# A one-element GpSimd copy that releases three held stores moves from in front of the last gather to behind it

## The chip, the cores and the metric

The kernel runs on one core of a Trainium2 chip. The metric is the device time of one execution in microseconds (us). Engines are named as in the profile: PE (TensorE matmul) and PEld (its weight load), DVE (VectorE), ACT (ScalarE), POOL (GpSimd) and SP (SyncE, which issues plain DMAs). A name with q behind it, as POOLq, is the engine's sequencer. Times on the axis of the trace count from the start of the span.

## The reference

Two layers, for 4 batches of 6208 tokens with 256 channels, in float32:

```
sig = 1 / (1 + exp(-f_logit))
f   = lower_bound + (1 - lower_bound) * sig
h_t = f_t * h_(t-1) + (1 - f_t) * x_t           # a scan over the tokens, per channel
y   = all h_t

scores = y @ w_gate                              # per batch: the 128 tokens of the highest score
h   = relu(y[top] @ w1)                          # 256 -> 1024
out = y;  out[top] = y[top] + sigmoid(scores[top]) * (h @ w2)
```

## The kernel before, in words

Tokens lie along the free axis and channels on the partitions. A batch is cut into units of up to four blocks of 256 tokens; there are 25 units, numbered 0 to 24, and batch 3 ends with unit 24. For each unit SP loads the gate logits and x, ACT makes the gates, POOL and DVE weigh x, DVE runs the scan, PE adds up the scores and turns the result so that tokens stand on partitions, ACT and DVE copy it out of PSUM into a tile `ym`, and SP stores this tile (1 MB for a unit of four blocks) to the output of its batch, line 446.

After the last unit of a batch its 128 best tokens are searched. Then comes the batch's expert step: a **gather** by indirect DMA on POOL (`fetch`, line 657) reads the chosen rows back from the output in device memory into `xe`; PE transposes them (line 685); the gate is a dot product on DVE (line 707); up matmuls (line 718 for the last batch, 727 for others), a relu on ACT (line 735), down matmuls (740, for the last batch 745), the mix with the gate on DVE (752, for the last batch two halves, 749), and a **scatter** by indirect DMA on POOL (line 756) that writes the rows back. The gather has to wait until the stores of its rows have landed, and the scatter until all stores of its batch have.

The stores of the last two units of batches 0 and 1 (units 5, 6, 11 and 12) are **held**: the stores of all other units go first. The gathers of these two batches leave out the rows of held units and take these from the tiles on the chip, so only the scatters of batches 0 and 1 wait for the held stores: batch 0's for unit 6, batch 1's for unit 12. `stored` is the order of all stores, `unheld` its first part. Unit 5 is the first of the held, and it is issued right behind unit 24's store. Units 6, 11 and 12 wait in addition for `("passed",)`. That is a copy of one element of unit 6's `ym` tile onto itself, on POOL: SP's next store reads this tile, so it waits for the copy, and the two behind it in SP's order wait with it.

The order on each engine is written by a planner (`Plan.run`) before the kernel is built. Each operation is given to it by `add(engine, cost, emit, rank, after, key, ...)`; of the operations that are ready on an engine the planner takes the smallest rank, at times that it works out from the costs. Here `p0` is 20 times the batch's last unit plus a constant of the batch, which is larger for batch 3 than for the batches before it; the scatter of batch 2 has a smaller rank than the copy and the gather of batch 3. The conditions (`after`) order the plan alone; on the chip an instruction waits for the tiles and tensors that it reads and writes. The copy is given the conditions of the last gather, the landing of unit 24's store among them, but it touches no more than its one element.

Before the last gather POOL also writes one element of each of batch 3's tiles (`see`, line 642) and so waits for the stores of units 19 to 23. The planner allows for the gather's landing on its own account, with `LAND[3]` = 1.85 and 0.36 for the queue, and 0.055 from one engine to the next. In the stretch between batch 2's matmuls and the down matmuls of the last batch the planner fills idle PE time with matmuls that nobody reads (line 967, `FILL` = 0.24 each), one for as long as more than 1.1 x `FILL` is free before the next real operation.

After the last batch's gate the engines read a flag and branch (lines 881 to 883): the usual case goes on with the same plan, the other case would search again. The scatters of batches 0, 1 and 3 stand behind this branch, in this order, and batch 2's ahead of it.

Of the kernel before, what the change touches and what calls it, by code (L numbers as in the profile page):

```python
# [53 lines left out]
HELD = [2, 2, 0, 0]  # L54
# [19 lines left out]
class Plan:  # L74
# [8 lines left out]
    def add(self, engine, cost, emit, rank, after, key=None, late=0.0, takes=(), load=1.0, over=None, behind=None, bank=()):  # L83
        if key is not None:
            self.at[key] = len(self.ops)
        if behind:
            self.behind[len(self.ops)] = behind
        self.bank[len(self.ops)] = [(name[:-2], name[-1] == "w") for name in ([bank] if isinstance(bank, str) else bank)]
        over = OVER.get(engine, 0.0) if over is None else over
        self.ops.append((engine, cost, emit, rank, [k for k in after if k is not None], late, takes, load * (cost - over), over))  # L90
# [179 lines left out]
def gated_scan_moe(tc, xf, heads_in, lbwg, w12, outs, cap):  # L270
    nc = tc.nc
    v, a, pe, g = nc.vector, nc.scalar, nc.tensor, nc.gpsimd
    with ExitStack() as ctx:
# [49 lines left out]
        for k in range(OWN):  # L323

            first = max(0, min(4, RANKED - 4 * k)) * LANE
# [18 lines left out]
        N = len(units)  # L344
        last_unit = {u[0]: i for i, u in enumerate(units)}
        first_unit = {u[0]: i for i, u in reversed(list(enumerate(units)))}
        held = {i for b in range(B) for i in range(last_unit[b] - HELD[b] + 1, last_unit[b] + 1)}
        unheld = [i for i in range(N) if i not in held]
        stored = unheld + sorted(held)
        before = dict(zip(stored[1:], stored))  # L350
        plan = Plan(SLOTS, CAPS)
        add = plan.add
        xs, fs, gs, pts, yms, wide, chosen, carry, aim, spelt = {}, {}, {}, {}, {}, {}, {}, {}, {}, {}
# [409 lines left out]
        def experts(b):  # L763
            st = {}
            fetch, turn_in, take, ask, opened, up, relu, down, mix, scatter = stages(b, st)
            turn_half, take_half, up_half, down_half, mix_half, copy_indices, see = st["half"]
            halved = b == B - 1
            p0 = 20.0 * last_unit[b] + EXPERT[b]
            k = lambda *t: ("moe", b, *t)

            prev = ("mix", b - 1)
            if halved:
                add("pool", 0.19, copy_indices, p0, [("st", b)], ("index", b))
                for i in range(last_unit[b - 1] + 1, N - 1):
                    add("pool", 0.17, lambda i=i: see(i), p0, [("store", i), ("store", "tail", b), ("index", b), ("seen", i - 1)], ("seen", i))
            ahead = [("st", b), ("index", b), ("seen", N - 2) if halved else None, ("store", last_unit[b] - HELD[b]), ("store", "tail", b)]
            if halved and len(stored) > len(unheld) + 1:
                first = stored[len(unheld) + 1]
                add("pool", 0.12, lambda: g.tensor_copy(yms[first][:1, 0, :1], yms[first][:1, 0, :1]), p0, ahead, ("passed",))
                ahead = [*ahead, ("passed",)]  # L780
            add("pool", 1.1, fetch, p0, ahead, k("fetch"))
            add("sw", 0.36, None, p0 - 1e3, [k("fetch")], k("row" if HELD[b] else "xe"), late=LAND[b])
            if HELD[b]:
                spell, broadcast, match, pick, join = st["held"]
# [9 lines left out]
            if halved:  # L794
                plan.tile(("pm", b, -1), ("pt", "pt"), [("xT", b, 1)])
                for h in range(NH):
                    add("pe", 0.272, lambda h=h: turn_half(h), p0 - 2, [k("xe"), ("moe", b - 1, "down", NF - 1), k("flip", h - 1)], k("flip", h), takes=[("pm", b, -h)], load=0.7, over=0.12)
                    add("dve" if h else "act", 0.28, lambda h=h: take_half(h), p0 - 2, [k("flip", h)], ("xT", b, h) if h else ("xT", b))
            else:
                add("pe", 0.438, turn_in, p0, [k("xe"), ("moe", b - 1, "down", NF - 1)], k("flip"), takes=[("pm", b, 0)], load=0.7, over=0.13)  # L800
                add("act", 0.375, take, p0 - 1, [k("flip")], ("xT", b))
# [174 lines left out]
        first = [("scores", first_unit[b], 0) for b in range(B)]  # L976
# [16 lines left out]
        for b in range(B):  # L993
            choose(b)
            experts(b)
# [37 lines left out]
```

## Time and profile before

| | |
|---|---|
| median of 3 runs | 208.09 us (207.54 to 208.29) |
| profiled execution | 207.37 us, of which the span is 205.5 us |
| mean granted clock of PE | 0.988 |
| PE, DVE, ACT, POOL busy | 183.3, 161.0, 155.8, 142.0 us |
| DMA | 79.64 MB, mean 388 GB/s |

The span runs from the first to the last instruction of the traced execution; the time of an execution is a little longer than its span. Busy time is the time in which an engine worked on instructions; the DMA figures count the packets of the core's 16 DMA engines. Idle time of an engine costs nothing where another sets the pace.

### The profile page before, as it was taken

The page shows a single profiled execution, that of the slowest core. Times are in us where ns is not written, and L with a number is a line of the kernel's source. Part 1 is how long each engine was busy: PE and PEld are TensorE (multiplying, and loading weights), DVE is VectorE, ACT ScalarE, POOL GpSimd, SP SyncE. Part 2 cuts the span into 40 slices and gives each one's busy share as a digit, 9 for nine tenths or more (in the row PEclk, how much of TensorE's full clock was granted, in tenths as well). Part 3 has the DMA queues.
Part 4 walks back from the last instruction along what each step waited for, and adds up shares of the span by engine and source line. Part 5 has one row for each costly group of instructions (what it writes and reads, how often), then busy time and mean ns, then how long its engine had stood idle before and what let it go on. Part 6 is the DMA issues. An engine that isn't in the chain of part 4 may idle for free. (4 is left out here: it accounts for less than half of the span.)

```text
span 205.5 us, 4047 instructions
## 1 busy us (share of the span) xinstructions
PE 183.3 (89%) x1561; PEld 136.8 (67%) x1561; DVE 161.0 (78%) x194; ACT 155.8 (76%) x205; POOL 142.0 (69%) x142
## 2 busy tenths in 40 slices
PE   5799999889798979999999999989989999990990
PEld 3577667566565757679876668769857666780990
DVE  0959999995998899999979999999999988500110
ACT  2788899967989968979999999997999983310210
POOL 5203996745999999994999999749969950322301
PEclk9999999999999999999999999999999999999698
DMA  5999999999999999999999999999999999999101
GB/s 191 390 443 427 427 401 444 427 429 427 411 423 418 420 442 409 438 419 421 418 442 407 427 405 429 413 435 416 437 426 405 427 427 425 420 419 389 64 26 35
DMA packets 9799, 79.64 MB, mean 388 GB/s; under 512 B 1329, under 2 KB 1597, under 8 KB 2736
## 3 DMA queue, kind: packets, MB, share of 16 engines
q1 hardware_dynamic: 9248, 78.39, 91.2%
q0 software_dynamic: 384, 0.95, 1.2%
q8 instruction: 14, 0.23, 0.5%
q14 instruction: 9, 0.07, 0.1%
q10 hardware_dynamic: 144, 0.00, 0.0%
HBM read 53.48 MB, written 25.95 MB: 387 GB/s over the span
## 5 line engine op out<-in xcount | busy, mean ns | idle before, releaser
L419 DVE TENSOR_TENSOR_SCAN whole<-gt,whole 128x1024 f32<-128x1024 f32 (+1 forms) x42 | 96.6, 2314 | 3.0 <-POOL whole L407 1.8
L407 POOL TENSOR_TENSOR whole<-whole 128x1024 f32<-128x1024 f32 (+6 forms) x41 | 79.3, 1949 | 8.0 <-ACT whole L395 7.7
L372 PE MATMUL pt<-ident,whole 128*128 128x128 f32 x384 | 58.8, 291 | 3.5 <-ACT whole L443 2.9
L372 PEld LDWEIGHTS pt<-ident,whole 128*128 128x128 f32 x384 | 48.4, 195 | 20.0 <-ACT whole L443 12.4
L399 ACT ACTIVATE gt<-whole,nl 128x1024 f32<-128x1024 f32 (+2 forms) x50 | 54.8, 1097 | 6.3 <-DVE whole L419 4.2
L443 ACT COPY whole<-pt 128x512 f32<-128x512 f32 (+1 forms) x90 | 49.2, 588 | 9.6 <-PE pt L372 9.5
L403 POOL TENSOR_SCALAR whole<-whole,nl 128x1024 f32<-128x1024 f32 (+6 forms) x41 | 38.8, 954 | 21.8 <-DMA whole<-xf 21.7
L395 ACT ACTIVATE whole<-whole 128x2048 f32<-128x2048 f32 (+2 forms) x25 | 46.3, 1851 | 0.6 <-DMA whole<-xf 0.5
L971 PE MATMUL score<-slot,ones 128*128 128x256 bf16 x306 | 41.0, 284 | 1.9 <-POOL slot L304 1.9
L971 PEld LDWEIGHTS <-ones 128*128 128x128 bf16 x306 | 30.8, 102 | 8.1 <-issue 2.5
L428 PE MATMUL score<-whole,wgr 128*32 128x256 f32 x384 | 31.3, 390 | 4.8 <-DVE whole L419 4.0
L416 DVE SCALAR_TENSOR_TENSOR whole<-gt,whole 128x1024 f32<-128x1024 f32 (+7 forms) x21 | 18.4, 875 | 3.7 <-ACT gt L399 3.7
L428 PEld LDWEIGHTS score<-whole,wgr 128*32 128x32 f32 x384 | 8.8, 108 | 13.4 <-DVE whole L419 7.8
L419 DVE TENSOR_TENSOR_SCAN whole<-gt,tl,whole 128x1024 f32<-128x1024 f32 (+1 forms) x8 | 15.3, 1937 | 0.3 <-POOL whole L407 0.2
L673 PE MATMUL acc<-whole,hT 128*128 128x256 f32 x64 | 14.8, 384 | 0.0
L756 POOL DMA_INDIRECT out<-res,aim x4 | 4.0, 1003 | 14.0 <-issue 6.7
L673 PEld LDWEIGHTS acc<-whole,hT 128*128 128x128 f32 x64 | 11.8, 190 | 2.4 <-DVE hT L669 1.0
L580 POOL TENSOR_SCALAR hot<-slot,rank 128x128 bf16<-128x128 bf16 x14 | 8.4, 605 | 5.6 <-DVE junk L567 5.4
L727 PE MATMUL pm<-xT,wt 128*128 128x128 f32 x96 | 11.5, 278 | 0.0
L735 ACT ACTIVATE hT<-pm 128x512 f32<-128x512 f32 x8 | 4.8, 595 | 8.8 <-PE pm L727 4.6
L727 PEld LDWEIGHTS pm<-xT,wt 128*128 128x128 f32 x96 | 11.0, 192 | 0.4 <-ACT open L711 0.4
L567 DVE TENSOR_SCALAR_CACHE_REDUCE junk<-acc,mine 128x448 bf16<-128x448 f32 x12 | 8.0, 665 | 0.2 <-PE acc L546 0.2
(128 smaller groups left out, 132.1 us busy)
## 6 DMA issues: line engine op xcount, KB each, us to landing
whole<-xf SPq DMA_DIRECT2D x15, 2048.0 KB, 16.1
out<-whole SPq DMA_DIRECT2D x23, 1024.0 KB, 17.8
whole<-xf SPq DMA_DIRECT2D x16, 1024.0 KB, 20.0
wt<-w SPq DMA_DIRECT2D x1, 2048.0 KB, 20.6
whole<-xf SPq DMA_DIRECT2D x2, 768.0 KB, 7.0
out<-whole SPq DMA_DIRECT2D x1, 768.0 KB, 11.5
tl<-heads SPq DMA_DIRECT2D x1, 512.0 KB, 4.2
whole<-xf SPq DMA_DIRECT2D x2, 256.0 KB
```

The source lines that it names most:

```text
L372: pe.transpose(out, src, ident)
L395: a.activation(fs[i], fs[i], ACTF.Sigmoid, scale=-1.0)
L399: a.activation(gs[i, h][:, :n], fs[i][:, h], ACTF.Identity, scale=nl[:, h : h + 1], bias=1.0)
L403: g.tensor_scalar(xs[i][:, h, c0:], xs[i][:, h, c0:], nl[:, h : h + 1], 1.0, ALU.mult, ALU.mult)
L407: g.tensor_tensor(xs[i][:, h, c0:], xs[i][:, h, c0:], fs[i][:, h, c0:], ALU.mult)
L416: v.scalar_tensor_tensor(xs[i][:, h, :c1], gs[i, h][:, :c1], 1.0, xs[i][:, h, :c1], ALU.subtract, ALU.mult)
L419: v.tensor_tensor_scan(xs[i][:, h], gs[i, h][:, :n], xs[i][:, h], carry[h] if blk0 else tl[:, 1, h, b, TAIL - 1 : TAIL], ALU.mult, ALU.add ...
L428: pe.matmul(score[j * CG : (j + 1) * CG, b % 2, c0:], wgr[:, h, CG - 1 - r : 2 * CG - 1 - r], src, start=(h == 0 and blk0 + q < 3), stop=( ...
L443: (v.tensor_copy if eng == "dve" else a.copy)(out, src)
L673: pe.matmul(acc[:, :D], st["hits"][:, c], yms[last_unit[b] - k][:, c], start=(k == 0 and c == 0), stop=(k == HELD[b] - 1 and c == NF - 1))
L727: pe.matmul(st["pm", f // TP][:, c : c + P], w1t[:, h, f * P : (f + 1) * P], st["xT"][:, h], start=(h == 0), stop=(h == NH - 1))
L971: pe.matmul(score[:, h].rearrange("p (k c) -> p k c", k=2), ones, slot.unsqueeze(1).to_broadcast([P, 2, P]), start=not begun, stop=True, s ...
```

## The change

The copy leaves its place in front of the last gather. It is now given to the planner behind it, with the gather's issue as its one condition and a rank 2 smaller than the gather's, in the branch of the code that only batch 3 takes. The gather no longer has the copy among its conditions. Nothing else is edited: the held stores 6, 11 and 12 still wait for `("passed",)`.

```
-            ahead = [("st", b), ("index", b), ("seen", N - 2) if halved else None, ("store", last_unit[b] - HELD[b]), ("store", "tail", b)]
-            if halved and len(stored) > len(unheld) + 1:
-                first = stored[len(unheld) + 1]
-                add("pool", 0.12, lambda: g.tensor_copy(yms[first][:1, 0, :1], yms[first][:1, 0, :1]), p0, ahead, ("passed",))
-                ahead = [*ahead, ("passed",)]
-            add("pool", 1.1, fetch, p0, ahead, k("fetch"))
+            add("pool", 1.1, fetch, p0, [("st", b), ("index", b), ("seen", N - 2) if halved else None, ("store", last_unit[b] - HELD[b]), ("store", "tail", b)], k("fetch"))
...
+                if len(stored) > len(unheld) + 1:
+                    first = stored[len(unheld) + 1]
+                    add("pool", 0.12, lambda: g.tensor_copy(yms[first][:1, 0, :1], yms[first][:1, 0, :1]), p0 - 2, [k("fetch")], ("passed",))
```

## Rows read from the trace of the kernel before

**Rows 1.** The page, the DMA engines' busy tenths in 40 slices.
```profile
DMA  5999999999999999999999999999999999999101
```

**Rows 2.** POOL's timeline, 178 to 206 us: start, us, engine, line, operation, idle before.
```profile
179.86 0.17 POOL L779 COPY whole<-whole 1x1 f32<-1x1 f32 x1
...
182.56 1.10 POOL L657 DMA_INDIRECT xe<-out,idx  x1 [2.52 <-DMA out<-whole]
...
193.00 1.00 POOL L756 DMA_INDIRECT out<-res,aim  x1 [6.43 <-issue]
194.31 0.98 POOL L756 DMA_INDIRECT out<-res,aim  x1 [0.30 <-issue]
...
200.67 0.99 POOL L756 DMA_INDIRECT out<-res,aim  x1 [5.38 <-POOLq L883]
```

**Rows 3.** The same timeline, SP's last issues, merged.
```profile
180.06 2.49 SPq L446 DMA_DIRECT2D out<-whole  x3
```

**Rows 4.** The store line, windows 174:176 and 180.35:180.5: durations, first and last issue, landing.
```profile
L446 SPq DMA_DIRECT2D out<-whole x2: 332/547/762, 174.1 to 174.5; - x2
...
DMA to landing us min/median/max: 8.2/9.2/10.3
...
L446 SPq DMA_DIRECT2D out<-whole x2: 332/580/828, 180.1 to 180.4; - x2
...
DMA to landing us min/median/max: 7.2/8.4/9.6
```

**Rows 5.** The gather's line over the whole span, four gathers, start to landing.
```profile
DMA to landing us min/median/max: 6.5/7.4/7.9
```

**Rows 6.** DMA queues in windows 183.66:187, 187.5:191, 191:193, 193:195.5: packets, MB, share.
```profile
q1 hardware_dynamic: 197, 1.43, 102.2%
...
q1 hardware_dynamic: 119, 0.83, 57.0%
q0 software_dynamic: 87, 0.24, 17.2%
...
q1 hardware_dynamic: 9, 0.04, 5.1%
q8 instruction: 1, 0.02, 3.8%
...
q0 software_dynamic: 48, 0.13, 14.7%
```

**Rows 7.** The timeline, 178 to 206 us, PE and DVE from the expert step on.
```profile
181.04 3.62 PE L740 MATMUL py<-wt,hT 128*128 128x256 f32 x16
...
184.50 0.81 PE L967 MATMUL warm<-slot,ones 128*128 128x512 bf16 x3
184.78 0.48 DVE L752 SCALAR_TENSOR_TENSOR res<-py,open,xe 128x256 f32<-128x256 f32 x1 [6.99 <-PE py L740]
...
190.11 0.41 PE L685 MATMUL pm<-ident,xe 128*128 128x128 f32 x2 [4.81 <-DMA xe<-out,idx]
...
190.82 5.31 PE L718 MATMUL pm<-xT,wt 128*128 128x128 f32 x32
...
199.80 0.35 DVE L749 SCALAR_TENSOR_TENSOR res<-acc,open,xe 128x128 f32<-128x128 f32 x1 [1.26 <-PE acc L745]
```

**Rows 8.** Busy time by stretch: us, the engines, granted clock, DMA share, GB/s.
```profile
190.55:193.90 3.35, 3.35 (x15) 3.08 (x15) 0.69 (x4) 0.42 (x2) 0.90 (x1) 0.50 0.10 37
```

**Rows 9.** The up matmuls of batch 2: ns min/median/max, first and last start.
```profile
L727 PE MATMUL pm<-xT,wt x32: 275/275/356, 177.4 to 180.9; 128*128 128x128 f32 x32
```

**Rows 10.** The scatter's line, windows 194.2:194.5 and 200.6:201: start to landing.
```profile
DMA to landing us min/median/max: 2.4/2.4/2.4
...
DMA to landing us min/median/max: 3.4/3.4/3.4
```

**Rows 11.** SP's timeline, its first issue; and DMA queues of 0:2, busy tenths by 0.05 us.
```profile
0.74 0.39 SPq L909 DMA_DIRECT2D tl<-heads  x1
...
DMA  0000000000000000000000000000000000099368
```

**Rows 12.** The branch after the flag, window 191.5:192.5.
```profile
L883 POOLq COMPARE_BRANCH  x1: 40/40/40, 191.9 to 191.9; - x1
```

## The prediction, on record before the changed kernel was run

> **What bounds the kernel now.** I read the page first. Its busy shares are means over stages with different limits, so the slices count: the DMA engines stand at 9 almost to the end and at 1 or 0 in the last three [rows 1]. So for most of the span the kernel is bound by moving data, which the change does not touch, and the end is a stage of its own, in which little data moves. What this stage is worth is read there.
>
> Second, GpSimd's timeline of the end [rows 2]. The reader is to see the order: the small copy at 179.86 (0.17 us), then a wait of 2.52 us for a store, and the last gather at 182.56. The copy needs no store of its own, so it runs 2.7 us before the gather, although the plan asks for the same conditions for both. SyncE's row answers at once: three stores from 180.06 on [rows 3], 0.03 us after the copy's end (179.86 + 0.17). These are units 6, 11 and 12, 1 MB each.
>
> Third, what is in flight. The store of unit 24, on which the gather waits, was issued at 174.1 and landed 8.2 us later, at 182.3; the one of unit 5 at 174.5, landing at 184.8; units 6 and 11 land at 187.3 and 190.0 [rows 4]. They land 2.5 and 2.7 us apart: a file of stores, 2.6 us each.
>
> Fourth, the gather itself. Its instruction ends at 183.66 (182.56 + 1.10), and the transposes on TensorE wait for its landing until 190.11, 7.5 us after its start [rows 2, 7]; the four gathers land after 6.5 to 7.9 us, 7.4 in the median [rows 5]. The queues' packets tell why: from 183.66 to 187 the software queue moved none, while the hardware queue moved 1.43 MB; from 187.5 to 191, as the stores run out, the software queue moved 87 [rows 6]. A scatter on free engines moved 48 packets within 2.5 us of its start [rows 6] and another landed in 2.4 us [rows 10]. So the gather stands behind the released stores for 4 to 5 us.
>
> Fifth, the timeline from there [rows 7]: transposes at 190.11, the up matmuls from 190.82, the down matmuls, the last mix until 200.15, the last scatter at 200.67, and 4.83 us from its start to the end of the span (205.5). TensorE pays once more: after standing idle from 185.3 to 190.1, its granted clock is 0.50 from 190.55 to 193.9, the lower of its two levels (1.2 GHz) [rows 8].
>
> **The change, part by part.** *Taken out ahead of the gather:* one copy of 0.17 us. It lies within the 2.52 us in which the gather waits for unit 24's store [rows 2], so this gains nothing; without that cover it would be worth 0.17 us.
>
> *Put behind the gather:* the same copy, and with it three store issues on SyncE. Does the planner really put it next? It is ready when the gather's issue ends, and so is the scatter of batch 2, which has the smaller rank, once its mix is done. TensorE's order answers this for the plan of before: three fillers stand between batch 2's down matmuls and the last transposes [rows 7]. The planner puts one in for each 0.24 us as long as more than 0.264 us is free, so it counts on 0.74 to 0.98 us there. It puts the transposes 0.36 + 1.85 + 0.055 = 2.27 us behind the gather, so, if nothing else holds the transposes, the gather ends 1.3 to 1.5 us before the down matmuls do, and the mix is later still. On the chip it is the same: gather over at 183.66, mix over at 185.26 [rows 2, 7]. So the copy comes right behind the gather: 183.66, plus nothing to 0.3 us (as between two scatters, 194.31 less 193.00 and 1.00); I take 0.15, and it ends at 184.0. Behind it on GpSimd stands the scatter of batch 2, which waits for its mix until 185.26 anyway. Behind the stores on SyncE stands only the end. The release is 4.0 us later than at 180.03.
>
> *The gather's landing.* Its start stays at 182.56, since unit 24's store is ahead of all held stores in its queue. A gather on free engines isn't in this trace. From below the nearest row is the scatter that landed in 2.4 us, then the last scatter with 3.4 [rows 10]; from above the quickest of the gathers among traffic with 6.5 [rows 5]. Once unit 5's store has gone, the engines have nothing else until the held stores' first bytes. Those need about 1.0 us from issue: the first load of the kernel was issued at 0.74 and moved its first packet at about 1.75 [rows 11]. So they come at 185.0, and the gather is nearer to the scatters than to gathers among traffic: I take 2.9 us, the middle of the two, landing at 185.46. Transposes at 185.5 (the fillers end at 185.3), 4.6 us earlier.
>
> *The clock.* With 0.2 us of idle in place of 4.8, TensorE should keep 1.00. The same 32 up matmuls of batch 2 at 1.00 go from 177.4 to 181.2 (3.75 us), these took 5.31 [rows 7, 9]: 1.56 us more. By this chain the last scatter would start at 200.67 - 4.6 - 1.56 = 194.5.
>
> *What is late next.* The last scatter stands on GpSimd behind the scatters of batches 0 and 1, which wait for units 6 and 12. Unit 12 lands at 184.0 + 1.0 (first bytes) + 3 x 2.6 (the spacing of landings) + the time from last bytes to landing. No row shows that time; it is bounded by nothing from below, and from above by unit 12 of before: by the spacing it lands at 190.0 + 2.6 = 192.6, and its bytes are nearly over by 191 (0.83 MB of the queue before, 0.04 MB after [rows 6]), which leaves 1.6 us. That is the nearest row, so I take 1.5: 194.3. Then batch 1's scatter at 194.4 (0.1 behind its wait) for 0.98, 0.3 to the next, and the last scatter at 195.7. That is later than 194.5, so the held stores set the end.
>
> *Sum.* End at 195.7 + 4.83 = 200.5 in place of 205.5: 5.0 us less. The profiled execution took 207.37 beside its span of 205.5, and the median of the runs shown is 208.09, 0.7 above it; I take the 5.0 us off the median: **203.1 us**.
>
> **The rivals.**
>
> *The last expert's own chain ends it.* If the stores land 1.2 us sooner (no lag behind the last bytes to speak of), the last scatter starts at 194.5, or at 194.2 if the gather lands in 2.4 us and the fillers hold the transposes until 185.3. That is 6.2 to 6.4 us less: 201.8. For it: engines that start empty have no backlog. Against it: the 1.6 us that unit 12 took at the end, when hardly anything else moved.
>
> *Code arrives behind the stores.* GpSimd branches at 191.9, a block of instructions is moved (the packet of the instruction queue between 191 and 193), and its next scatter starts at 193.00, 1.1 us on [rows 2, 6, 12]. The branch follows the transposes by 1.8 us, so it comes at 187.3, amid the held stores. If this block waits as the gathers did, up to 7.9 us [rows 5], the scatters start at 195.2, 196.5 and 197.8, and the end is at 202.6, 2.9 us less than before: 205.2. The Trainium skill ("Runtime: NRT & Kernel Launch", "Instruction fetch mechanics") says that a taken branch out of the fetched window must wait for a DMA of the target; [rows 6] agree that a block is moved there, and no row shows one that waits under load.
>
> *Slower: two code blocks in turn.* The same place, and each of two blocks waits its 7.9 us: the first scatter would start at 187.3 + 15.8 = 203.1, the last at 205.7, the end 5.0 us later, 213. It turns into a loss once the first of the three scatters starts after 198.1. Against it: the stores' bytes are over at about 192.8, and from then on a block costs 1.1.
>
> *No change: the gather's 7.4 us are its own.* All four gathers take 6.5 to 7.9 us [rows 5]. If this is the cost of fetching scattered rows, nothing ahead of the last scatter moves, unit 12 lands at 194.3, in time for 200.67, and the time is 208.1. Against it: no packet of its queue before 187 and then 87 [rows 6], and the scatters' 2.4. The Trainium skill ("DMA: Bandwidth & Descriptors", "Queues, rings and completion order") says that each DMA engine takes turns between queues, packet by packet; by this rule the gather would have had its turn from 183.7 on, and moving the stores would buy nothing. The trace disagrees: it had no turn for over 3 us [rows 6].
>
> *The copy isn't next.* If the planner puts batch 2's scatter ahead of it, the copy waits for that mix (185.26 [rows 7]) and a scatter's 1.0 us: it runs at 186.4 in place of 183.8, the last scatter starts at 198.3, and 2.4 us are left of the gain: 205.7. TensorE's three fillers speak against it.
>
> **How the numbers follow.** Likeliest (203.1) 0.55; the expert's chain (201.8) 0.17; code behind the stores (205.2) 0.13; no change (208.1) 0.07; two blocks (213) 0.05; the copy behind the scatter (205.7) 0.03. Within 0.5%, 1.04 us, a measurement can't tell this kernel from no change. Faster: 0.55 + 0.17 + 0.13 + 0.03 = 0.88; same 0.07; slower 0.05. The range from 201.5 (the quickest gather) to 206.0 holds the first three and the last, and the bounds of the gather's landing and of the lag; a clock that stays at 0.50 leaves 196.1 for the last scatter, 203.5, within it too.
>
> **What would show it.** The copy directly behind the gather on GpSimd; three stores at about 184.0; packets of the software queue between 183.7 and 185, none later for the gather; transposes at 185.5; a granted clock of 1.00 through the up matmuls, in 3.75 us; batch 1's scatter waiting for unit 12, and the last one right behind it, at 195.7. It is wrong if the gather still lands 6 us after its start, if GpSimd stands without reason after its branch, or if the last scatter follows its mix and not batch 1's scatter.

## The result, and the profile after

| | before | after |
|---|---|---|
| median of 4 runs each | 208.19 us (207.54 to 208.31) | 202.82 us (202.3 to 203.15) |
| span of the profiled execution | 205.5 us | 200.8 us |
| mean granted clock of PE | 0.988 | 0.996 |

The ratio is 0.9746, with a 95% interval from 0.9714 to 0.9778: faster by 2.5%. The forecast was 203.1 us.

GpSimd's timeline of the end, in the changed kernel (start, us, engine, line, operation, idle before):

```profile
182.75 1.10 POOL L657 DMA_INDIRECT xe<-out,idx  x1 [2.52 <-DMA out<-whole]
183.85 0.18 POOL L796 COPY whole<-whole 1x1 f32<-1x1 f32 x1
...
186.77 1.03 POOL L756 DMA_INDIRECT out<-res,aim  x1 [2.74 <-DVE res L752]
...
190.02 1.00 POOL L756 DMA_INDIRECT out<-res,aim  x1 [2.21 <-issue]
...
194.89 0.98 POOL L756 DMA_INDIRECT out<-res,aim  x1 [3.87 <-DMA out<-whole]
196.18 0.99 POOL L756 DMA_INDIRECT out<-res,aim  x1 [0.30 <-DMA xe<-out,idx]
```

Against [rows 2], the gather starts at the same time after the same wait, and the copy now begins the moment the gather's instruction ends. Batch 1's scatter, at 194.89, no longer follows batch 0's by 0.3 us: it waits 3.87 us for a store, and the last scatter stands right behind it. SyncE answers the copy at once:

```profile
184.06 2.69 SPq L446 DMA_DIRECT2D out<-whole  x3
```

The gather's line (its landing), and then the DMA queues of two windows, 182.9 to 185 and 185 to 187:

```profile
DMA to landing us min/median/max: 3.6/3.6/3.6
```
```profile
q0 software_dynamic: 24, 0.09, 18.9%
q1 hardware_dynamic: 14, 0.08, 9.4%
q8 instruction: 1, 0.02, 3.2%
...
q1 hardware_dynamic: 101, 0.83, 97.5%
q0 software_dynamic: 24, 0.04, 6.8%
```

The gather's 48 packets now move ahead of and beside the first held bytes, where [rows 6] show none before 187. It lands 3.6 us after its start, not 7.5. The expert step follows, from the same timeline:

```profile
182.27 3.62 PE L740 MATMUL py<-wt,hT 128*128 128x256 f32 x16
...
185.73 0.59 PE L965 MATMUL warm<-slot,ones 128*128 128x512 bf16 x2
186.01 0.48 DVE L752 SCALAR_TENSOR_TENSOR res<-py,open,xe 128x256 f32<-128x256 f32 x1 [6.99 <-PE py L740]
...
186.53 0.41 PE L685 MATMUL pm<-ident,xe 128*128 128x128 f32 x2 [0.20 <-DMA xe<-out,idx]
...
187.24 3.84 PE L718 MATMUL pm<-xT,wt 128*128 128x128 f32 x32
...
194.74 0.35 DVE L749 SCALAR_TENSOR_TENSOR res<-acc,open,xe 128x128 f32<-128x128 f32 x1 [1.26 <-PE acc L745]
```

The stretch of the up matmuls (us, then PE, PEld, DVE, ACT, POOL, granted clock, DMA share, GB/s):

```profile
187.24:191.08 3.84, 3.84 (x34) 3.84 (x35) 0.42 (x4) 0.80 (x2) 1.57 (x2) 1.00 1.02 429
```

The transposes come 3.58 us earlier (190.11 less 186.53). The 32 up matmuls run at clock 1.00 and take 3.84 us where they took 5.31 [rows 7, 8]: 1.47 us. The last mix starts at 194.74 for 199.80, 5.06 us earlier, which is these two together. The last scatter starts only 4.49 us earlier (200.67 less 196.18): 0.57 us went to batch 1's scatter, which waited for unit 12. The span is 4.7 us shorter. Meanwhile the DMA engines, nearly idle in this stage before [rows 8], move 429 GB/s: the held stores have gone under the expert's matmuls.

### The profile page after: what moved, and what is told of

It is laid out like the page before. It is cut to its first block, busy times and chain, and to the rows that moved or that the text cites. A ratio compares the mean times of both kernels' runs of the same rounds, so it can differ in the third digit from the quotient of the medians.

```text
span 200.8 us, 4045 instructions
## 1 busy us (share of the span) xinstructions
PE 180.5 (90%) x1560; PEld 134.5 (67%) x1560; DVE 161.1 (80%) x194; ACT 155.5 (77%) x205; POOL 141.8 (71%) x142
## 5 line engine op out<-in xcount | busy, mean ns | idle before, releaser
L969 PE MATMUL score<-slot,ones 128*128 128x256 bf16 x306 | 39.9, 279 | 1.9 <-POOL slot L304 1.9
L969 PEld LDWEIGHTS <-ones 128*128 128x128 bf16 x306 | 30.2, 100 | 7.3 <-issue 2.2
```

The costliest lines, as they stand in the source:

```text
L969: pe.matmul(score[:, h].rearrange("p (k c) -> p k c", k=2), ones, slot.unsqueeze(1).to_broadcast([P, 2, P]), start=not begun, stop=True, s ...
```

## The experiments

Ratios are to the kernel before, run on the same chip as the experiment. In each of the three groups the kernels ran on one chip.

### Is it the release of the stores, or the copy's place on GpSimd?

*two_copies*: the changed kernel keeps the old copy in front of the gather as well.

```
+            ahead = [("st", b), ("index", b), ..., ("store", "tail", b)]
+            if halved and len(stored) > len(unheld) + 1:
+                first = stored[len(unheld) + 1]
+                add("pool", 0.12, lambda: g.tensor_copy(...), p0, ahead, ("early",))
+                ahead = [*ahead, ("early",)]
...
                     add("pool", 0.12, lambda: g.tensor_copy(...), p0 - 2, [k("fetch")], ("passed",))
```

> The changed kernel with the old copy kept in front of the gather as well; the held stores wait for the second copy, behind the gather. My theory (only the release of the stores matters, the copy itself lies in the gather's wait for unit 24's store): as the changed kernel, 202.8 us within 0.5, the gather landing about 3.6 us after its start. Rival (what the copy in front does to GpSimd or to the gather's own start is part of the gain): between 203.5 and 208.

Measured: 203.29 us, ratio 0.9767 (0.9719 to 0.9815), the gather landing 2.9 us after its start. So the copy in front costs nothing that can be measured; it is the release that counts.

*no_copy*: the kernel before without a copy, so that the condition that the stores have on it is void.

```
-                add("pool", 0.12, lambda: g.tensor_copy(...), p0, ahead, ("passed",))
```

> The kernel before without any copy: nothing holds units 6, 11 and 12 back but the order of SyncE. My theory (a gather stands behind the store bytes that were handed over ahead of it, and it doesn't matter whether that was 3 or 7 us ahead): as the kernel before, 208.2 us within 1, the gather landing 7 to 8 us after its start, transposes at about 190. Rival (the place of the copy on GpSimd costs, not the stores): 202.8.

Measured: 208.24 us, ratio 1.0035 (1.0002 to 1.0068), between no change and 0.7% more. From its timeline, and then the gather's landing:

```profile
176.01 4.59 SPq L446 DMA_DIRECT2D out<-whole  x4
...
190.53 0.66 PE L685 MATMUL pm<-ident,xe 128*128 128x128 f32 x2 [3.94 <-DMA xe<-out,idx]
```
```profile
DMA to landing us min/median/max: 7.3/7.3/7.3
```

The last of these four issues came at 179.4, and at 181.3 in the kernel before; the gather fares the same. The old copy did nothing for it.

### Are the bytes of the held stores the whole cost?

*small_after* and *small_before*: in the changed kernel and in the one before, units 6, 11 and 12 store only one partition of their tile (8 of 1024 rows; the other rows of these units stay unwritten). The copy, the waits and the three issues remain.

```
+                r = 1 if i in stored[len(unheld) + 1 :] else P
-                nc.sync.dma_start(outs[b][t0 : t0 + n, :].rearrange("(p c) d -> p (c d)", p=P),
-                                  yms[i].rearrange("p c d -> p (c d)"))
+                nc.sync.dma_start(outs[b][t0 : t0 + r * cols, :].rearrange("(p c) d -> p (c d)", p=r),
+                                  yms[i][:r].rearrange("p c d -> p (c d)"))
```

> The changed kernel, which stores of units 6, 11 and 12 only the tile's first partition (8 rows of 1024); the other rows of these units are left out. It shows what the held stores still cost in the changed kernel. My theory (they hold the last scatter by way of batch 1's scatter, 0.6 us later than 0.5 us after its mix, and load the gather a little): 0.6 to 1.3 us under the changed kernel, 201.5 to 202.2, the last scatter 0.5 us behind the last mix. Rival (they cost nothing any more): 202.8. A gather on free engines is seen here by itself: I expect 2.9 to 3.6 us from start to landing.

> The kernel before with the same small stores of units 6, 11 and 12 (8 rows of 1024 each, the rest left out), released in front of the gather. My theory (bytes ahead of the gather are the whole cost of the old order): as the changed kernel with small stores, 201.5 to 202.2, granted clock 1.00 in the up matmuls. Rival (the gather takes 6.5 to 7.9 us of its own when a copy and store issues stand ahead of it): near 207.

Measured: 202.17 us, 0.9712 (0.9664 to 0.9761), and 202.21 us, 0.9714 (0.9662 to 0.9767). Without the bytes the two orders are one and the same. From the timeline of the kernel before with small stores, and its gather's landing:

```profile
183.19 1.10 POOL L658 DMA_INDIRECT xe<-out,idx  x1 [2.39 <-DMA out<-whole]
...
186.82 0.38 PE L686 MATMUL pm<-ident,xe 128*128 128x128 f32 x2
...
195.88 0.99 POOL L757 DMA_INDIRECT out<-res,aim  x1 [3.90 <-POOLq L884]
```
```profile
DMA to landing us min/median/max: 2.9/2.9/2.9
```

A gather on engines that are nearly free lands after 2.9 us, the value that the forecast took. The rival by which its 7.4 us are its own is dead. What the held stores still cost in the changed kernel is at most small: 202.17 against 203.29 of two_copies on the same chip, with intervals that overlap.

### How much does each store ahead of the gather cost?

*one_ahead* and *two_ahead*: unit 6, or units 6 and 11, no longer wait for the copy; the rest still does.

```
-("passed",) if i in stored[len(unheld) + 1 :] else None
+("passed",) if i in stored[len(unheld) + 2 :] else None
...
-                if len(stored) > len(unheld) + 1:
-                    first = stored[len(unheld) + 1]
+                if len(stored) > len(unheld) + 2:
+                    first = stored[len(unheld) + 2]
```

> The changed kernel with unit 6 no longer held: 1 MB of the 3 goes ahead of the gather, units 11 and 12 wait for the copy behind it. The engines were nearly idle from 182.7 to 185 in the changed kernel, which is about one such store (2.5 us at 419 GB/s). My theory: the gather stands behind that store and lands 0.5 to 1.5 us later, unit 12 lands 2.0 to 2.6 us earlier, so the last scatter now follows its own mix by 0.5 us, at about 196.1 to 197: 202.8 to 203.8 us. Rival (the file of held stores sets the end alone): 2 us less than the changed kernel, 200.8.

> The same with units 6 and 11 ahead of the gather, only unit 12 behind it. My theory (each MB handed over ahead of the gather costs it about 2.5 us once the idle time is used up): the gather lands 2.5 to 3.5 us later than in the changed kernel, the transposes start at about 189.5, the granted clock may fall to 0.50 for part of the up matmuls: 205.5 to 207.5 us. Rival (the gather shares the engines with whatever is queued, so one or two stores ahead cost it little): 202.8 or less.

Measured: 204.92 us, 0.9841 (0.9797 to 0.9885), and 206.97 us, 0.9945 (0.9916 to 0.9974). First the landing of one_ahead's gather and its transposes, then the same of two_ahead:

```profile
DMA to landing us min/median/max: 5.0/5.0/5.0
```
```profile
188.39 0.66 PE L685 MATMUL pm<-ident,xe 128*128 128x128 f32 x2 [3.13 <-DMA xe<-out,idx]
```
```profile
DMA to landing us min/median/max: 6.7/6.7/6.7
```
```profile
189.96 0.66 PE L685 MATMUL pm<-ident,xe 128*128 128x128 f32 x2 [4.58 <-DMA xe<-out,idx]
```

None, one, two and three stores ahead: the gather lands after 2.9 to 3.6, 5.0, 6.7 and 7.5 us. The second kernel came out within what was expected; the first was missed by 1.1 us. I had counted on the idle time of the engines to take up one store, with 0.5 to 1.5 us for the gather. It was 1.4 to 2.1 us, and TensorE idled 3.13 us for it, so part of the up matmuls ran at half clock:

```profile
189.00:191.00 2.00, 2.00 (x10) 1.76 (x9) 0.69 (x4) 0.40 (x2) 0.00 (x0) 0.50 0.93 381
```

They took 4.91 us in place of 3.84.

### Do the held stores set the end now?

*late_release*: five operations on a spare 128x128 tile stand between the gather and the copy on GpSimd.

```
+                    def release():
+                        spare_row = moe.tile([P, P], BF16, name="spare_row")
+                        for _ in range(5):
+                            g.tensor_scalar(spare_row, slot, 1.0, None, ALU.is_equal)
+                        g.tensor_copy(yms[first][:1, 0, :1], yms[first][:1, 0, :1])
...
-                    add("pool", 0.12, lambda: g.tensor_copy(...), p0 - 2, [k("fetch")], ("passed",))
+                    add("pool", 0.12, release, p0 - 2, [k("fetch")], ("passed",))
```

> The changed kernel with five GpSimd operations on a spare 128x128 tile between the gather and the copy, some 0.6 us each, so that the stores are released about 3 us later; nothing else waits for these operations. My theory (batch 1's scatter waits for unit 12, and the last scatter stands behind it): all of it comes through, unit 12 lands about 3 us later and the time is 205.2 to 206.2 us, with the transposes and the last mix where they were or 0.5 us earlier. Rival (the last expert's own chain sets the end): 202.8.

Measured: 205.09 us, 0.9858 (0.9805 to 0.9912), 0.1 us below the range. Its timeline:

```profile
186.37 2.85 SPq L446 DMA_DIRECT2D out<-whole  x3
...
193.29 0.35 DVE L749 SCALAR_TENSOR_TENSOR res<-acc,open,xe 128x128 f32<-128x128 f32 x1 [1.26 <-PE acc L745]
...
197.14 0.97 POOL L756 DMA_INDIRECT out<-res,aim  x1 [4.24 <-DMA out<-whole]
198.41 0.98 POOL L756 DMA_INDIRECT out<-res,aim  x1 [0.30 <-DMA out<-res,aim]
```

The stores go out 2.31 us later than in the changed kernel (186.37 less 184.06), and the last scatter starts 2.23 us later (198.41 less 196.18), although the last mix comes 1.45 us earlier and has ended 4.8 us before its scatter starts. So the last expert's chain doesn't set the end here, and the rival is dead. How much of a later release arrives at the end is less sure. Against after_again, whose rows stand below, the stores go out 2.08 us later and the last scatter starts only 0.92 us later: from the release to batch 1's scatter it is 10.8 us here and in the changed kernel's first profile, and 11.9 us in after_again and two_copies. By the medians, 205.09 us against 202.82 and 203.09 on other chips, it is 2.0 to 2.3 us.

### Can the rest be won?

*after_again* is the changed kernel once more, for comparison. *last_first* puts the last batch's scatter ahead of batch 1's. *dve_release* lets VectorE do the copy, as soon as unit 24's store has landed, beside the gather's issue and not behind it.

```
-    *([("moe", c, "scatter") for c in range(b) if HELD[c]] if halved else [])
+    *([("moe", 0, "scatter")] if halved else [("moe", B - 1, "scatter")] if b == 1 else [])
```
```
+                    def release():
+                        v.memset(yms[N - 1][:1, 0, :1], 0.0)
+                        v.tensor_copy(yms[first][:1, 0, :1], yms[first][:1, 0, :1])
...
-                    add("pool", 0.12, lambda: g.tensor_copy(...), p0 - 2, [k("fetch")], ("passed",))
+                    add("dve", 0.2, release, p0 - 2, [k("fetch")], ("passed",))
```

> The changed kernel itself, unedited, for a comparison with the two beside it on the same chip: 202.8 us within 0.8.

> The changed kernel with the last batch's scatter put ahead of batch 1's on GpSimd, so that it no longer stands behind unit 12; batch 1's scatter now comes last. My theory (the end is the later of the last mix plus 0.5 and unit 12's landing, and then two scatters that can't overlap): the last mix and unit 12 come within 1.5 us of one another in the profiles so far, so this moves the time by -1 to +0.7 us, 201.8 to 203.5. Rival (batch 1's scatter alone holds the end): the whole of what the small stores gained, 0.7 us or more less.

> The changed kernel with the release on VectorE: one element of unit 24's tile is set to 0 after its store has landed, then the copy of unit 6's element, so that the stores go out as the gather begins, about 1.2 us earlier than from behind it. My theory (the held stores set the end by 0.6 to 2 us, but the gather loses as soon as store bytes are queued ahead of it; 1 MB ahead cost it 1.4 to 2.1 us): unit 12 lands 1.2 us earlier, the gather lands 0.5 to 2 us later, the time is 202.3 to 204.3. Rival (the gather only suffers from stores issued well ahead of it): 0.6 to 1.2 us less than the changed kernel.

Measured: after_again 203.09 us, 0.9785 (0.9748 to 0.9821); last_first 202.67 us, 0.9755 (0.9728 to 0.9782); dve_release 207.31 us, 0.9977 (0.9952 to 1.0002). The order of the scatters is worth too little to be told apart: in last_first the last batch's scatter starts at 195.22 and batch 1's at 196.50, where after_again has

```profile
194.34 0.35 DVE L749 SCALAR_TENSOR_TENSOR res<-acc,open,xe 128x128 f32<-128x128 f32 x1 [1.26 <-PE acc L745]
...
196.20 0.98 POOL L756 DMA_INDIRECT out<-res,aim  x1 [5.56 <-DMA out<-whole]
197.49 0.99 POOL L756 DMA_INDIRECT out<-res,aim  x1 [0.30 <-DMA out<-res,aim]
```

dve_release was missed by 3 us, to the bad. Its timeline:

```profile
182.51 0.14 DVE L799 COPY whole<-whole 1x1 f32<-1x1 f32 x1 [4.54 <-issue]
...
182.68 1.77 SPq L446 DMA_DIRECT2D out<-whole  x3
182.74 1.10 POOL L657 DMA_INDIRECT xe<-out,idx  x1 [2.62 <-DMA out<-whole]
...
190.09 0.66 PE L685 MATMUL pm<-ident,xe 128*128 128x128 f32 x2 [4.82 <-DMA xe<-out,idx]
```

And its DMA queues, from the end of the gather's instruction at 183.84 to 188, and from 188 to 190:

```profile
q1 hardware_dynamic: 224, 1.69, 104.6%
...
q1 hardware_dynamic: 97, 0.66, 79.9%
q0 software_dynamic: 48, 0.13, 16.4%
```

A release 1.38 us earlier than in the changed kernel (182.68 for 184.06) gives nearly the whole gain back: the gather has no packet before 188. Only some 0.3 MB of the held stores had moved by 184 (the hardware queue moved 0.46 MB from 182 to 184, and 0.17 in the changed kernel), but the issues of all three had begun by 183.5, before the gather's instruction ended. So what counts is which transfer is issued first, not how long before, and the rival is dead too. The order isn't a strict one: from 188 to 190 the gather's 48 packets move beside 0.66 MB of the stores, with as much of these still to come until 192, and [rows 6] show the like from 187.5 on. This fits the third store ahead adding little, 0.5 to 0.8 us (6.7 to between 7.2 and 7.5), where the first added some 2 and the second 1.7.

## Why the prediction was right

**The gather stood behind the released stores.** Right, and shown: without their bytes it lands in 2.9 us in either order, with one, two or three stores ahead in 5.0, 6.7 and 7.5. What failed is what the prediction made of the rule of the Trainium skill ("DMA: Bandwidth & Descriptors", "Queues, rings and completion order") that each engine takes turns between queues, packet by packet: the gather did not have its turn at once, and had none for over 4 us after its instruction's end in dve_release. The rule itself isn't refuted by this. By the same section of the Trainium skill a turn is a whole packet of about 9 to 17 descriptors; the 224 packets that the profile counts there are 14 for each of the 16 engines, so if each of them is one descriptor, a single turn may cover them (an estimate from that section's figure). Whether the gather's own descriptors lay ready all that time, no run here shows.

**The copy and its old cover.** Right: the gather starts at 182.75 after the same 2.52 us of waiting, and two_copies is as fast.

**The copy comes next on GpSimd.** Right, at 183.85, with no gap (0.15 us were taken); the stores at 184.06.

**The gather's landing.** 2.9 us were taken and measured in four of the profiles that release behind it or store little; 3.0 in two, and 3.6 in the one shown, where half of its packets moved beside the first held bytes. With its start 0.19 later this put the transposes at 186.53, not 185.5. The landing alone isn't the whole of this: TensorE's down matmuls for batch 2 came 1.23 us later than in the kernel before (182.27 for 181.04), and the fillers behind them ended at 186.32 where the prediction had 185.3, so a landing after 2.9 us would have brought the transposes only to 186.3. This start differs from profile to profile, from 180.97 in late_release to 183.02 in small_after; the sum had no term for it.

**The clock.** Right: 1.00 through the up matmuls, 1.47 us for the 1.56 forecast.

**What is late next.** Right in kind: unit 12, through batch 1's scatter, holds the last one. Its terms were off in size. Unit 12 was to land at 194.3, and batch 1's scatter to start 0.1 us behind. The sequencer's row of the scatter's line, from 192 to 200, shows when GpSimd's wait for the stores was over, at the first of two semaphore events:

```profile
L756 POOLq EVENT_SEMAPHORE  x2: 17/30/43, 194.1 to 194.9; - x2
```

So in this profile unit 12 landed at 194.1, 0.2 us ahead of the forecast, and batch 1's scatter started 0.8 us behind it, at 194.89. The 0.1 taken for this step is the term that put the last scatter at 196.18, not 195.7. In after_again and two_copies the wait was over at 195.4 and 195.3, and the scatter again started 0.8 us later. There the store's own row gives the landing too: issued at 185.1 and landed 10.2 us later. That the landing came out so well in the first profile is luck, for two errors cancel in it. The term that no row showed, 1.5 us from the last bytes to the landing, was too long: the hardware queue has no packet after 193.75 in the changed kernel, and none after 194.97 in after_again, so it is about 0.4 us. Its upper bound of 1.6 was misread, since the last 9 packets behind 191 [rows 6] went on to 192.4. And the last bytes, which the spacing of 2.6 us put at 192.8, came 0.9 us later, and 2.2 in after_again; why they did, stays open.

**The tail behind the last scatter.** Taken as 4.83 us, it was 4.62 (200.8 less 196.18) and 4.2 in after_again (201.7 less 197.49). It isn't a constant. Its varying part is the last scatter's own landing: 3.4 us after its start before [rows 10], 3.1 in the changed kernel, 2.6 in after_again; in all twelve profiles the span ends 1.4 to 1.6 us behind that landing. A last scatter 0.5 us late and a tail 0.2 short partly cancel; that the median came out 0.3 us from the forecast owes something to this, and is in so far luck.

**The rivals.** *The expert's chain ends it*: nearly so in the profiled run, where batch 1's scatter adds 0.57 us, and not so in after_again, where the last mix has ended 2.8 us before its scatter starts. *Code behind the stores*: not seen. The flag's branch and load in the changed kernel:

```profile
L881 POOLq COMPARE_BRANCH  x2: 40/40/41, 188.9 to 196.2; - x2
```
```profile
L880 POOLq TENSOR_LOAD <-total x1: 1119/1119/1119, 187.7 to 187.7; - x1
```

The first scatter behind the branch starts at 190.02, 1.1 us on, just as before and amid the stores, and with it the two-block rival falls. Its premise had been misread as well: between branch and scatter no packet of an instruction queue starts, neither in the kernel before nor in the changed one. These are all the queues of the windows 191.9 to 193 before and 187.9 to 190.2 after:

```profile
q1 hardware_dynamic: 2, 0.01, 1.9%
...
q1 hardware_dynamic: 133, 0.97, 100.3%
```

The packet of [rows 6] started between 191 and 191.9, ahead of the branch. So these 1.1 us aren't shown to be a block's, and how long a branch would wait for a block amid the stores, no run here shows. *No change* and *the copy isn't next* are answered above.

## What to carry to other kernels

Before a small transfer on which an engine waits, look at what is already handed to the DMA engines, not only at what the issuing engine waits for: a gather of 0.13 MB behind 3 MB took 7.5 us in place of 2.9, and TensorE's half clock after the wait cost 1.5 us more. Tie the release of bulk stores that nobody waits for yet to the issue of the urgent transfer itself, as an instruction behind it on its own engine (an event 1.4 us earlier lost the gain), and then ask what waits for the delayed stores in turn: here a release 2.3 us later still made the kernel some 2 us slower.

## What the runs showed of the hardware that had not been expected

- For 4 us one queue had the engines to itself: in dve_release the hardware queue moved 1.69 MB from 183.84 to 188 and the software queue nothing, although the gather's instruction was over at 183.84 and the three stores had begun to be issued only 1.2 us before. In two_ahead packets of both moved side by side, 32 of the software queue and 106 of the hardware queue from 186 to 188.
- Loading the flag into GpSimd's registers took 1.12 us amid the held stores, and 0.51 us in the kernel before, with the engines nearly idle.
- TensorE's last branch, at the end of the program, took 3.47 us before and 3.74 after; in the changed kernel it ends at 199.5, 1.3 us ahead of the end of the span and 0.2 us behind the landing of the last scatter (196.18 and 3.1). In after_again it ends at 198.8, 1.3 us ahead of that landing, and the span still ends 1.6 us behind the landing, so the tail isn't seen to hang on this branch.
